# The third unit's first MLP matmul by block products, and a new step plan for three units

## The chip, the cores and the metric

The kernel runs on one core of a Trainium2 chip. The core has five engines that run at the same time and meet through semaphores: TensorE (PE, matmuls into PSUM), VectorE (DVE, elementwise), ScalarE (ACT, elementwise with activation functions), GpSimd (POOL, elementwise, slower) and SyncE (SP, whose queue here does nothing but start DMA transfers). Each engine takes its instructions in the order of its own queue. Time is device time in microseconds (us); lower is better.

## The reference

Two blocks, one after the other. The first is a gated linear recurrence over 768 steps, for 4 batches and 8 heads of 48 dimensions:

```python
f = 1.0 / (1.0 + np.exp(-f_logit))
for t in range(S):
    state = f[:, :, t, :, None] * state + np.einsum('bhd,bhe->bhde', k[:, :, t], v[:, :, t])
    y[:, :, t] = np.einsum('bhd,bhde->bhe', q[:, :, t], state)
```

Its output, laid out as x with 3072 tokens of 384 features, goes through an MLP with 2048 hidden features, all in float32:

```python
h = x @ w_in
g = h * (1.0 / (1.0 + np.exp(-1.702 * h)))
return g @ w_out
```

## The kernel before

**Units.** The 3072 tokens are cut into 12 units of 256 tokens, numbered 0 to 11 here; "the third unit" is unit 2. For each unit the kernel does the attention part and then the MLP part. The MLP of a unit runs beside the attention of the unit after it: its matmuls are the fill that keeps PE busy while DVE, ACT and POOL prepare the next step of the attention.

**Attention of a unit.** q, k and f are loaded raw, transposed (by DVE from unit 2 on, L382) into X and F, and f goes through a sigmoid (ACT L412, POOL L409). POOL multiplies neighbouring gates into `tot` (L457). Six levels of scores follow, two at a time (`levels`, L599): PE makes the scores `sc` (L466), DVE "promotes" q and k by the gates (L564), ACT copies parts aside (`Kc` L535, `Qc` L541), and DVE evacuates the scores into A (L507, L526). Then PE makes y from A and v (L584), the new states from kn and v (L695), DVE chains the states (L717 to L721), and PE adds the state's share to y (L742). ACT copies y out (L757), and DMAs on SP's queue turn it into the tile xT that the MLP reads (L815, L820).

**The MLP of units 0 and 1** is plain: h of 128 hidden features is three matmuls of 256 columns, one for each third of x (L1173, `mlp_h`), ACT applies the activation (L1177), and o is summed over blocks of four hidden tiles (L1187, added by DVE at L1243). While this goes on the weights arrive. They are loaded in 16 pairs of tiles of 64-bit floats (`fetch_weights`, L208) and turned into float32 by one ACT instruction (L252) and three DVE steps (L248, L241, L251). The loads have three buffers.

**The MLP of units 3 to 11** is by block products (`mlp_h20`, L1042). The matrix w_in is seen as 4 rows of 3 blocks, x as 3 blocks of features by 2 halves of tokens; the 24 block products are replaced by 20 products of sums of blocks, in the manner of Strassen. A product is four matmuls of 128 columns (L1079). Its left side is a sum of blocks of w_in (c1, p3, p7 and so on), made once: some stand in tiles of their own (`sums_of_w`, N_...), some overwrite a block of w_in in place (`sums_in_place`, L1002). Its right side is a sum of blocks of x, twelve sums for each unit, made by POOL (`sums_of_x`, L1037, the tiles E). The products are added up by chaining them in PSUM, by ACT copies (L1086, L1094, L1098) and by DVE adds (L1107), and activated by ACT (L1098, L1109). The products come in the order of `WHOLE` (L958): 18, 0, 7, 2, 17 and so on, of which number 18 needs the sum s7, the first that POOL makes, number 0 needs q0, the fourth, and 2 needs w, the sixth. The second matrix is done by seven products of quarters in the same manner (`mlp_o7`, L883, from unit 2 on), whose sums of w_out (T) DVE makes at L851, and whose sums of g it makes at L872 to L881.

**Unit 2 before the change** has the plain h (48 matmuls of 256 columns), run from its last block of hidden features to its first, and the o by seven products. Between its blocks stand the in-place sums (`mlp_unit`, L1224 to L1227): as soon as h has read a row of w_in for the last time, that row may be overwritten.

**Order.** PE and POOL take the instructions in the order in which the program writes them; DVE, ACT and SP too up to `fill_order.close()` (L1434), and afterwards a scheduler orders those three, except where `issue_after` puts one instruction behind another. For the attention of units 1, 2 and 3 what stands between the parts is written out by hand in `PLAN` (L1415), and inside the levels of unit 2 in `HOLES` (L276). A letter is a step: f takes the next item of the fill (for plain h the three matmuls of a tile; else one matmul of o, or one product), c is one step of a weight conversion, p begins the next conversion, w starts the next weight load on SP's queue, s takes the next of the waiting sums (`chores`), k is an idle matmul. From unit 4 on `merge` (L1304) spreads the fill by a rule.

The steps go through this function:

```python
def follow_steps(steps):
    for step in steps:
        if step == "f":
            fill.pop(0)[1]()
        elif step == "c":
            convert()
        ...
        elif step == "s":
            for job in chores[:1]:
                chores.remove(job)
                job()
```

## Time and profile before

| what | value |
|---|---|
| median of 3 runs | 575.57 us (575.4 to 575.83) |
| the profiled execution's own time | 575.35 us |
| its span | 573.6 us |
| PE busy | 563.7 us (98%) |
| DVE busy | 441.2 us (77%) |
| ACT busy | 291.7 us (51%) |
| POOL busy | 144.5 us (25%) |
| unit 2's plain h on PE (L1173) | from 142.74 to 165.39 us, with one pair of scores inside |
| unit 3's products on PE (L1079) | from 189.23 to 208.38 us, with one pair of scores inside |
| from unit to unit in the steady part | 43 us (the h of units 4 and 5 end at 251.56 and 294.56) |

A line of the order of time reads: start in us, length in us, engine, line of the kernel, instruction, output tile and input tiles, their shapes, how many instructions are merged into the line, and in brackets how long the engine had been idle before and what ended that. SPq, ACTq and PEq are the queues of those engines, where a DMA is started. Each float32 matmul shows as two PE records.

### The profile page before, as it was taken

What the parts mean: (1) busy time and instruction counts of PE and PEld (TensorE: products, weight loads), DVE (VectorE), ACT (ScalarE), POOL (GpSimd) and SP (SyncE); (2) the same over time, 40 slices, a digit from 0 to 9 for tenths busy, and PEclk for the clock granted to TensorE, in tenths of its full rate; (3) what the DMA queues carried; (4) which work ended last, traced back from release to release, by engine and by line L of the source; (5) the groups of instructions that cost most, each with busy time, mean ns of one, the idle gap of its engine ahead of it and who ended that gap; (6) DMA issues with size and microseconds to landing.
All of it is one profiled execution on the core that took longest, in us unless ns stands there. A gap on an engine that the chain in (4) does not pass through costs nothing.

```text
span 573.6 us, 18612 instructions
## 1 busy us (share of the span) xinstructions
PE 563.7 (98%) x7876; PEld 516.7 (90%) x7876; DVE 441.2 (77%) x695; ACT 291.7 (51%) x592; POOL 144.5 (25%) x227
## 2 busy tenths in 40 slices
PE   8899999999999999999999999999999999999997
PEld 7767777786899999999999999999999999999996
DVE  2899688988997786887887888886888886462294
ACT  4755553432553573564564564564564573543440
POOL 4030220419451601601601601601501601303000
PEclk9999999999999999999999999999999999999999
DMA  7869595932362452363453353453362121001000
GB/s 180 207 183 228 138 261 133 246 79 77 84 163 68 120 139 57 85 172 76 109 129 71 97 130 88 113 127 71 97 158 44 49 57 30 30 2 29 29 1 28
DMA packets 85939, 60.01 MB, mean 105 GB/s; under 512 B 33441, under 2 KB 77633, under 8 KB 85857
## 3 DMA queue, kind: packets, MB, share of 16 engines
q1 hardware_dynamic: 85328, 58.21, 40.3%
q8 instruction: 62, 1.02, 0.8%
q10 hardware_dynamic: 529, 0.62, 0.4%
q14 instruction: 20, 0.16, 0.1%
HBM read 45.16 MB, written 8.91 MB: 94 GB/s over the span
## 4 chain that ended last, share of the span: by engine, by line
PE 90%; DMA 3%; DVE 2%; ACT 2%; issue 1%; SPq 1%; ACTq 0%; DVEq 0%
PE h L1079 28%; PE o_Y L937 14%; PE o_Z L937 9%; PE h L1173 9%; PE sc L466 6%; PE o L1187 6%; PE o_X L937 5%; PE o_W L937 4%; PE y L584 2%; PE y L742 2%; PE t L394 2%; PE sc L695 2%; DMA xT<-yT 1%; DVE X L564 1%; DMA bits<-in_moe_w_in_dram 1%
## 5 line engine op out<-in xcount | busy, mean ns | idle before, releaser
L564 DVE TENSOR_TENSOR X<-X,tot 128x1024 f32<-128x1024 f32 x50 | 69.0, 1381 | 40.7 <-PE sc L466 35.1
L535 ACT COPY Kc<-X 128x512 f32<-128x512 f32 x72 | 48.3, 671 | 85.6 <-DVE X L564 71.0
L1079 PE MATMUL h<-E,w_in 128*128 128x128 f32 (+1 forms) x648 | 82.6, 276 | 0.0
L1079 PEld LDWEIGHTS h<-E,w_in 128*128 128x128 f32 x648 | 77.1, 192 | 0.5
L1107 DVE TENSOR_TENSOR g<-g,h 128x512 f32<-128x512 f32 (+1 forms) x92 | 55.4, 628 | 25.9 <-PE h L1079 18.0
L1037 POOL TENSOR_TENSOR E<-xT 128x128 f32<-128x128 f32 (+1 forms) x36 | 16.0, 454 | 231.0 <-DMA xT<-yT 231.0
L1173 PE MATMUL h<-xT,w_in 128*128 128x256 f32 x288 | 65.6, 382 | 0.2 <-DMA xT<-yT 0.2
L1173 PEld LDWEIGHTS h<-xT,w_in 128*128 128x128 f32 x288 | 53.8, 190 | 9.3 <-DMA xT<-yT 0.6
L1109 ACT ACTIVATE g<-g 128x512 f32<-128x512 f32 (+1 forms) x70 | 40.3, 588 | 34.1 <-DVE g L1107 34.1
L937 PE MATMUL o_Y<-T,S 128*128 128x192 f32 x320 | 57.6, 329 | 0.0
L937 PEld LDWEIGHTS o_Y<-T,S 128*128 128x128 f32 x320 | 52.3, 190 | 0.5
L1187 PE MATMUL o<-w_out,g 128*128 128x384 f32 x128 | 44.3, 492 | 0.0
L1098 ACT ACTIVATE g<-h 128x512 f32<-128x512 f32 (+1 forms) x70 | 37.0, 550 | 12.9 <-PE h L1079 11.0
L382 DVE STREAM_TRANSPOSE X<-raw 128x512 f32<-128x512 f32 x38 | 40.9, 1115 | 1.5 <-PE y L742 1.0
L526 DVE COPY_PREDICATED A<-masks,sc 128x256 f32<-128x256 uint32 (+1 forms) x98 | 41.9, 503 | 0.0
L757 ACT COPY yT<-y 48x256 f32<-48x256 f32 (+1 forms) x66 | 22.0, 369 | 30.0 <-PE y L742 29.5
L1079 PE MATMUL h<-E,N_c 128*128 128x128 f32 (+1 forms) x288 | 37.1, 275 | 0.0
L1187 PEld LDWEIGHTS o<-w_out,g 128*128 128x128 f32 x128 | 23.6, 190 | 14.6 <-issue 0.7
L1079 PEld LDWEIGHTS h<-E,N_c 128*128 128x128 f32 x288 | 35.1, 192 | 0.2 <-DVE osb L897 0.2
L466 PE MATMUL sc<-X,Kc 48*64 48x64 f32 x1344 | 28.3, 220 | 3.0 <-ACT Kc L535 1.2
L1177 ACT ACTIVATE g<-h 128x256 f32<-128x256 f32 x48 | 17.7, 382 | 25.5 <-PE h L1173 25.2
L466 PEld LDWEIGHTS sc<-X,Kc 48*64 48x64 f32 x1344 | 24.1, 134 | 7.3 <-ACT Kc L535 3.1
(132 smaller groups left out, 1103.4 us busy)
## 6 DMA issues: line engine op xcount, KB each, us to landing
bits<-in_moe_w_out_dram SPq DMA_DIRECT2D x8, 768.0 KB
raw<-in_f_logit_dram SPq DMA_DIRECT2D x48, 96.0 KB
raw<-in_k_dram SPq DMA_DIRECT2D x48, 96.0 KB
bits<-in_moe_w_in_dram SPq DMA_DIRECT2D x8, 576.0 KB
raw<-in_q_dram SPq DMA_DIRECT2D x44, 96.0 KB
k_tok<-z SPq DMA_DIRECT2D x64, 64.0 KB
kt<-k_tok SPq DMA_DIRECT2D x16, 256.0 KB
out_dram<-osb SPq DMA_DIRECT2D x20, 192.0 KB
```

Of the source, the lines that this page charges most:

```text
L382: copied["turned"] = nc.vector.transpose(view(out, at, [[HALF, NP], [step, R4], [R4 * step, 32]]), by_half[:, j, f].rearrange("p a (j d) - ...
L466: nc.tensor.matmul(t["sc"][h][g * HS:(g + 1) * HS, a, s, :], lhsT=t["Kc", l][rows(h), x:x + HS], rhs=rhs(h, a, g), start=True, stop=True,)
L526: moved = nc.vector.copy_predicated(out=view(A, c * HALF + at, dims), mask=mask.bitcast(U32), data=got)
L535: nc.scalar.copy(c.rearrange("p (n two m) -> p n two m", two=2, m=m), view(X, KF * SLOT, [[2 * m, SLOT // (2 * m)], [(KR - KF) * SLOT + m, ...
L564: done = nc.vector.tensor_tensor(x, x, y, ALU.mult)
L937: nc.tensor.matmul(t[name], lhsT=lhs(f), rhs=rhs(f), start=(new and i == 0), stop=(i == HF - 1), skip_group_check=True,)
L1079: nc.tensor.matmul(ph[:, t], lhsT=WA[a][:, f // 2, f % 2 * P:(f % 2 + 1) * P], rhs=E[n][b], start=(root and t == 0), stop=not goes_on, ski ...
L1098: nc.scalar.activation(to, ph, AF.Copy, scale=float(sign))
L1107: copied["sum"] = nc.vector.tensor_tensor(to, to, part, ALU.add if sign > 0 else ALU.subtract)
L1109: nc.scalar.activation(to, to, AF.Gelu_apprx_sigmoid)
L1173: nc.tensor.matmul(ph, lhsT=w_in[:, ff // 2, c, ff % 2 * P:(ff % 2 + 1) * P], rhs=xTs[n][:, c, :], start=(c == 0), stop=(c == NK - 1))
L1187: nc.tensor.matmul(t["po"], lhsT=g[ff // FG][:, ff % FG, tt * P:(tt + 1) * P], rhs=w_out[:, ff, :], start=(ff == ffs[0]), stop=(ff == ffs[ ...
```

## The change

Unit 2's h is made by twenty block products like that of the units after it. For that:

- `mlp_unit` loses its special case for unit 2; the lanes of PSUM are taken from `turns` if no unit before has set them (L1114).
- The sums of w_in must be ready before unit 2's products. The sums in their own tiles are made during unit 2's attention (steps s; `more` hands out c1, c4, p12). After it, and ahead of unit 3's first part, POOL gets the four in-place sums k, p3, p1, p14, then p15 and p16 (three instructions), and DVE gets p7, p19 and p4, behind the last state step that was written. The other three in-place sums of DVE (p9, p5, p11) are chores of unit 3's plan, behind the promotion of unit 3's level 1.
- `sums_of_x(n)` is called without its condition n > N_FILL. So POOL makes unit 2's twelve sums; unit 0 comes to the same line and makes twelve as well, which nothing reads.
- `PLAN` for the three units and `HOLES` are written anew. Around the steps that matter: unit 1's plan takes one more item of fill ahead of its last y matmuls; unit 2's first level has three conversion steps, not one, between the copies aside and the first promotion, and one, not five, ahead of the second; the load of pair 9 stands ahead of unit 2's v loads, that of pair 11 behind eight raw loads; sixteen matmuls of o of units 0 and 1 stand behind unit 2's y and not thirteen; seventeen products of unit 2 follow on one another behind unit 3's last scores.
- The third weight pair's load is written one part earlier in the opening; the sums of w_out (T) lose their tie to a transpose.

From unit 5's attention on, PE's order of work is the same in both kernels.

```diff
-    HOLES = {(N_FILL, 0): "c", (N_FILL, 1): "cccffcfcw", (N_FILL, 2): "fcp", (N_FILL, 3): "cfcf", (N_FILL, 4): "fcwwff", (N_FILL, 5): "c"}
+    HOLES = {(N_FILL, 0): "ccc", (N_FILL, 1): "c", (N_FILL, 3): "cpccfwwff", (N_FILL, 4): "ccsw", (N_FILL, 5): "f"}
...
             half(1)
             xTs[n] = xT
-            if n > N_FILL:
-                sums_of_x(n)
+            sums_of_x(n)
...
         def sub(*x):
-            with ExitStack() as order:
-                if next(made) < 2:
-                    order.enter_context(tc.issue_after(copied["turned"].ins))
-                nc.vector.tensor_tensor(*x, ALU.subtract)
+            summed.append(nc.vector.tensor_tensor(*x, ALU.subtract))
...
+        third = ("p4", "c1", "-", "a30"), ("p15", "p15", "", "p4"), ("p16", "a20", "", "a21"), ("p16", "p16", "", "a22")
...
     def sum_of_w(engine, out, x, op, y):
 
-        if op == "-":
-            with tc.issue_after(copied["promoted"].ins):
+        with ExitStack() as order:
+            if engine == nc.vector:
+                order.enter_context(tc.issue_after(copied.get("promoted", copied["state"]).ins))
+            if op == "-":
                 engine.scalar_tensor_tensor(WA[out], WA[x], -1.0, WA[y], op0=ALU.mult, op1=ALU.subtract)
+            else:
+                engine.tensor_tensor(WA[out], WA[x], WA[y], ALU.add if op else ALU.subtract)
+
+    def sums_in_place(engine):
+
+        if engine == nc.gpsimd:
+            for out, at in (("p7", "a01"), ("p19", "a12"), ("p5", "a31"), ("p9", "a11"), ("p11", "a00")):
+                WA[out] = WA[at]
+            sums = (
+                ("k", "a02", "a02", "+", "a30"), ("p3", "a02", "a11", "", "k"), ("p1", "a32", "a21", "+", "c3"),
+                ("p14", "a10", "a10", "", "c2"),
+            )
         else:
...
+            sums = (
+                ("p7", "a01", "a11", "", "c3"), ("p19", "a12", "c2", "-", "a20"), ("p9", "a11", "c4", "", "a11"),
+                ("p5", "a31", "a31", "", "c3"), ("p11", "a00", "a00", "", "c1"),
+            )
...
-            free = lanes["o"]
+            free = lanes.get("o") or [next(turns) % 4 for _ in range(4)]
...
-        if n > N_FILL:
-            return mlp_h20(n, g, before) + o
-        by_block = {}
...
-        for r in reversed(range(NGR)):
-            items += mlp_h(n, range(r * FG, (r + 1) * FG), by_block)
-            if r:
-                items.append((0, lambda r=r: sums_in_place(r), 0))
-        return items + [(0, end, 0)] + o
+        return mlp_h20(n, g, before) + o
...
     PLAN = {
         3: (
-            "ffffffsfffsfff", "fffsf", "ffffs", "fffsfsfssfffff", "s", "f", "ffsffffff", "ffffffffff", "fffffsssf",
+            "sssfcfffsssfffffsffff", "sfffffff", "", "", "fffpfsffsffsffffffffffffffff", "f", "f",
+            "ffffffffffffffffffff", "ffff",
         ),
         1: (
-            "cccwcccwkkkkk", "kkkcf", "cfccwf", "fcffcwffcffcf", "ffcc", "f", "cwc", "fcc", "ff", "cff", "", "f",
-            "wffwfffff",
+            "cccwcccwkkkkk", "kkkcf", "cfccwf", "fcffcwffcffcf", "ffcc", "f", "cwc", "fcc", "cfff", "", "pw", "fff",
+            "wffffff",
         ),
         2: (
-            "ffffff", "fcfff", "fcffffccswfwpfcsf", "cfc", "ccfcffscsffcf", "ffffsffffffff", "f", "fffcffsffff",
+            "fffff", "ffcfffpcff", "sfcfffcfcsfcpccffwwfcs", "", "fffscfff", "scffscfssfscffffcfffffffcf", "",
+            "fpfffff",
         ),
     }
...
-    while chores:
-        chores.pop(0)()
+    by_pool, by_ve, rest = [*sums_in_place(nc.gpsimd)], [*sums_in_place(nc.vector)], [*more.pop()()]
+    for x in (*by_pool, *by_ve[:2], *rest):
+        x()
...
-    of_b = [*sums_of_b()]
-    for x in sums_of_w(("c1", "c4", "p12", "p4", "p16")):
-        chores += of_b[:1] + [x]
-        del of_b[:1]
-    chores += of_b
+    chores += by_ve[2:] + [*sums_of_b()]
```

## The prediction

> **What bounds the kernel now.** I read the page first (busy shares and slices), then the waits between 57 and 210 us, then TensorE in order of time over the stage that is edited, then the queue of GpSimd (POOL) over the same stage.
>
> ```profile
> PE 563.7 (98%) x7876; PEld 516.7 (90%) x7876; DVE 441.2 (77%) x695; ACT 291.7 (51%) x592; POOL 144.5 (25%) x227
> PEclk9999999999999999999999999999999999999999
> ```
>
> TensorE (PE) is busy for 98% of the span at the full granted clock, so a time comes down only if PE gets less to do, and comes down by less wherever PE then waits. The waits from 57 to 210 us, longest first (who waited for whom: us, times, longest):
>
> ```profile
> POOL w_in L1000 <- PE h L1173: 9.8, 3, 4.8
> ...
> PE sc L466 <- DVE A L526: 0.6, 1, 0.6
> ...
> PE sc L466 <- ACT Kc L535: 0.4, 1, 0.4
> ```
>
> PE has only two of its own in 153 us; POOL's 9.8 is the old in-place sums waiting for h to be through with each row of w_in, which costs nobody. PE in order of time:
>
> ```profile
> 85.27 0.69 PE L466 MATMUL sc<-Qc,Kc 48*64 48x64 f32 x32 [0.59 <-DVE A L526]
> ...
> 142.74 4.05 PE L1173 MATMUL h<-xT,w_in 128*128 128x256 f32 x18
> 146.72 0.69 PE L466 MATMUL sc<-Qc,Kc 48*64 48x64 f32 x32
> 147.83 0.69 PE L466 MATMUL sc<-X,Kc 48*64 48x64 f32 x32 [0.42 <-ACT Kc L535]
> 148.45 17.10 PE L1173 MATMUL h<-xT,w_in 128*128 128x256 f32 x78
> 165.39 2.11 PE L937 MATMUL o_Y<-w_out,g 128*128 128x192 f32 x12
> ...
> 189.23 1.95 PE L1079 MATMUL h<-E,N_c 128*128 128x128 f32 x16
> 191.11 0.69 PE L466 MATMUL sc<-Qc,Kc 48*64 48x64 f32 x32
> ...
> 192.20 2.05 PE L1079 MATMUL h<-E,w_in 128*128 128x128 f32 x16
> ...
> 208.38 2.77 PE L937 MATMUL o_Y<-w_out,g 128*128 128x192 f32 x16
> ```
>
> The reader sees the two forms of h side by side (the records show two instructions to a matmul): unit 2's by blocks of 256 columns, 142.74 to 146.72 and 148.45 to 165.39, and unit 3's by products, 189.23 to 191.11 and 192.20 to 208.38. The two waits are 0.59 us at 85.27 and, at 146.72, scores that take 1.73 us where this pair takes 1.09 at 191.11.
>
> POOL, which must now make unit 2's sums of x:
>
> ```profile
> 127.08 1.04 POOL L457 TENSOR_TENSOR tot<-F 128x512 f32<-128x512 f32 x1 [16.62 <-DVE st L720]
> 128.20 4.16 POOL L457 TENSOR_TENSOR tot<-tot 128x256 f32<-128x256 f32 x4
> 132.43 0.22 POOL L457 TENSOR_TENSOR D<-tot 128x16 f32<-128x16 f32 x1
> 132.61 3.50 POOL L1000 TENSOR_TENSOR N_c<-w_in 128x512 f32<-128x512 f32 x2
> ...
> 144.78 1.27 POOL L1000 TENSOR_TENSOR N_p<-N_p,N_p 128x512 f32<-128x512 f32 x1
> ...
> 227.49 0.87 POOL L1037 TENSOR_TENSOR E<-xT 128x128 f32<-128x128 f32 x2 [29.67 <-DMA xT<-yT]
> 228.43 1.32 POOL L1037 TENSOR_TENSOR E<-xT,E 128x128 f32<-128x128 f32 x1
> 229.83 0.87 POOL L1037 TENSOR_TENSOR E<-E,xT 128x128 f32<-128x128 f32 x2
> ```
>
> POOL is idle 75% of the span, but not here: from 127.08 it runs without a gap to 146.05.
>
> **The change part by part.** The sum is made in this profiled execution, 575.35 us with 573.6 us of span; the median of the runs shown is 575.57, 0.22 above it.
>
> *Unit 2's h.* Off PE: 48 matmuls of 256 columns, 3.98 + 16.94 = 20.92 us. Onto PE: 80 of 128 columns, by unit 3's rows 1.88 + 16.18 = 18.06. Gain 2.86 us. With it come ten adds on VectorE (DVE) of 685 ns and ScalarE copies and activations of 10.9 instead of 6.1 us. In unit 3 the same load sits beside 18 us of products with no PE wait, and the five in-place sums that DVE made in this stretch (0.71 to 1.39 us each) are made earlier, so I price them at nothing; without that cover the bank of a product comes free late, up to one add, 0.7 us.
>
> *Old waits.* The new plan has five fewer o matmuls ahead of the scores of 85.27, but VectorE no longer waits there for a pair of w_in that landed at 76.97: its load now goes ahead of unit 2's five v loads on SP's queue (3.2 us of issue), which wait one load's issue longer and are used at 91 us. So 0.59 goes. The 0.64 at 146.72 goes into the reckoning below. Together -1.23.
>
> *Ahead of unit 2.* Since the condition on the sums of x is gone, unit 0 makes twelve too, which nothing reads, when its xT lands at 39.3 us. POOL is free until 67.0, and the twelve take 7.3 us in unit 3 (184.15 to 191.49). What they can hold up is DVE: while POOL made tot at 29.05, a conversion step took 1.32 us at 29.18 where its row is 0.55 at 36.25. Four or five steps by 0.4 to 0.6 are 1.3 to 2.7 us, against the slack of the scores at 53.25 (Kc ready at 51.86, and 0.5 us of DVE idle before): bounds 0 to 0.8, taken 0.1, since the small sums cost less (0.96 against 0.55 at 30.42). Unit 1's y comes one o matmul (0.65 us) later, its xT landed at 69.12 and PE was there at 69.57, with 0.14 of issue: +0.35. Three conversion steps instead of one stand ahead of unit 2's first promotion (71.33, freed by Qc), 0.55 + 0.96 us more, twice that if POOL is at its sums: Kc at 74.2 to 75.0 against 74.4: 0 to 0.6, taken 0.2. Levels 2 to 5: the scores are ready 0.2 to 0.5 us ahead of PE by the same rows; 0 to 1.5, taken 0.05. Sum +0.7. On SP, pair 11's load now stands behind eight raw loads of f (7.4 us of issue at 74.61): it lands near 86.5, six us after issue as pair 9's at 70.98, and is converted near 89.5; the third pair's load, written earlier, keeps its place in the queue. Nothing for both, and the 1.5 just named if pair 11 is late.
>
> *POOL's queue ahead of unit 2's products.* Now the order on POOL is tot of unit 3, four sums in place, three more of w_in, then the twelve E. tot can't start before unit 2's last state step reads the old one, as in 127.08. The sums at their own rows: 2 x 1.61 (both inputs from w_in), 2 x 1.28, 1.27, 1.67, 1.89 and 0.07 between: 11.1. tot costs 3.2 (unit 4's, 194.63 to 197.82) to 5.6 (here); 4.4, the middle, is taken, because three VectorE sums run beside it where four longer instructions did. So E begins at 127.1 + 4.4 + 11.1 = 142.6. All uncontended, 3.2 + 7 x 1.27 + 0.5, gives 139.8; the pace of 127.08 to 144.78, the same seven sums and tot beside a full DVE, 144.8. PE, 0.1 us later up to here (0.7 less 0.59), comes to the first product at 142.8: 16 o matmuls (10.6) and scores (1.09) after the scores that ended at 132.96, less the three o matmuls (1.99) that stood ahead of these and now stand behind. The first product needs the first sum only (s7); the second needs the fourth (q0), 2.75 us after E begins by the rows at 227.49: 145.35, where PE would be at 143.7. Wait 1.65; the scores behind the third product need Kc, which ScalarE now copies behind an activation of the second, +0.15: 1.8. Bounds 0 (139.8) and 3.85 (144.8); 1.8 because own rows are nearer than a stretch with other DVE work. The three sums behind the promotion (p9, p5, p11) queue on DVE ahead of the next promotion: six w_in sums at 0.71 to 1.39 bring Kc to 146.8 to 148.5, PE wanting it at 147.7 after the wait; they cost only where POOL is early.
>
> *After it.* y now follows its h by one product of o more and the next h by one less: from the end of y to the first product are 24 o matmuls (7.8) and two pairs of scores (2.18), 9.98 us, where it was 13.3. E began 8.25 us after y's end (184.15 less 175.9), q0 is needed 0.9 after the first product: no wait if E is not contended, 0.2 if so. kn's second half: its transpose waits behind one more add. +0.1 for both, 0 to 1. From unit 5's attention on PE's order is the same.
>
> Sum: -2.86 - 1.23 + 0.7 + 1.8 + 0.1 = -1.5, 573.85 in the profiled execution, 574.1 beside the median.
>
> **A rule weighed.** The row: at 151.17 two DVE sums in w_in took 2.78 us together beside POOL's, and one alone at 157.64 took 0.71. The Trainium skill (SBUF — State Buffer, Who interferes with whom) says that a DVE instruction with two SBUF inputs and a GpSimd instruction that reads SBUF exclude each other for the whole instruction. By that rule DVE's and POOL's lists add up and the time is the slow rival's, 577.7, where the rows give 574.1; the trace agrees with the rule in part, as the rival's last figures show.
>
> **Rivals.**
> *POOL in time.* E at 139.8, no wait at the products: -2.86 - 1.23 + 0.7 + 0.1 = -3.3, 572.3 beside the median, as the rest here. For it: POOL's 1.27 rows. Against: DVE is 14.5 of 16.5 us busy here.
> *POOL and DVE strictly in turn (slower).* POOL 12.6 us uncontended, and DVE's two-input work in the same stretch, 6 sums of 0.71 and two promotions of 1.23, 6.7: E at 146.4, q0 at 149.15, PE waits 5.45 from 143.7: +2.2, 577.7. Before, from 127.08 to 146.05, POOL's rows uncontended are 13.4 and DVE's two-input work 9.5, yet 19.0 elapsed, not 22.9; three fifths of DVE's work counted, which puts E at 143.7. It decides the sign from E at 144.2, and is slower by over 0.2% from 145.4.
> *The plan's head pays.* Dead sums 0.8, Kc 0.6, levels 2 to 5 at 1.0: +2.75 with 0.35 for xT, instead of 0.7: 576.1. Against: each has slack in the trace.
>
> **How the numbers follow.** About 0.2% (1.15 us) is what a measurement of this kernel tells from no change. Forecast 0.45, at 574.1, own range 573.0 to 575.4: faster by over 0.2% up to 574.4, 0.30, the rest within. POOL in time 0.2, all faster. In turn 0.25, slower in 0.22. Plan's head 0.1, slower in 0.04, within in 0.06. So faster 0.50, same 0.24, slower 0.26. The range, 572.2 to 577.3, holds the forecast's, the fast case's centre, the plan's head and the slow case up to E at 146.0; some 0.2 is left out.
>
> **What would show it.** h of unit 2 as 160 L1085 records in about 18 us; no wait at the scores near 83; the E records of unit 2 starting near 142.6 and a wait on POOL at the second product of about 1.7; twelve E records near 40 us with stretched conversions beside them. I am wrong if E begins past 145.4, if the scores before 95 wait by over 1 us, or if unit 3's products wait for E.

## The result and the profile after

The changed kernel takes 579.32 us in the median of five runs (578.0 to 580.65), the kernel before 575.57 (five runs, 575.4 to 576.06): a ratio of 1.0058, 95% interval 1.0042 to 1.0074. In a second round it was 578.99 against 574.94, ratio 1.0069 (1.0054 to 1.0083). So it is slower by 0.6 to 0.7%, where the prediction had 574.1 and no more than 577.3.

The first line of the page of the changed kernel, then what PE waited for from 30 to 215 us (who waited for whom: us in total, times, longest):

```profile
PE 561.2 (97%) x7940; PEld 515.9 (90%) x7940; DVE 450.9 (78%) x705; ACT 295.2 (51%) x594; POOL 160.7 (28%) x251
```

```profile
PE h L1085 <- POOL E L1043: 1.6, 2, 1.2
PE sc L466 <- DVE A L526: 1.5, 2, 0.8
...
PE o L1193 <- ACT g L1183: 1.1, 1, 1.1
PE h L1179 <- ACT g L1183: 0.9, 1, 0.9
PE sc L466 <- ACT Kc L535: 0.8, 2, 0.5
```

PE has 2.5 us less to do than before (561.2 against 563.7), and the span is 2.5 us longer (576.1 against 573.6): PE stands idle 5 us more than before, twice what the products took off it. Where the waits stand, in PE's order of time (start, length, instruction, in brackets the idle time ahead of it and what ended it):

```profile
48.88 2.85 PE L1193 MATMUL o<-w_out,g 128*128 128x384 f32 x8 [1.08 <-ACT g L1183]
...
75.34 0.70 PE L466 MATMUL sc<-X,Kc 48*64 48x64 f32 x32 [0.27 <-ACT Kc L535]
...
82.36 1.56 PE L1179 MATMUL h<-xT,w_in 128*128 128x256 f32 x6 [0.94 <-ACT g L1183]
...
92.48 0.69 PE L466 MATMUL sc<-Qc,Kc 48*64 48x64 f32 x32 [0.82 <-DVE A L526]
...
143.03 0.69 PE L466 MATMUL sc<-Qc,Kc 48*64 48x64 f32 x32 [0.64 <-DVE A L526]
...
146.68 1.16 PE L1085 MATMUL h<-E,N_c 128*128 128x128 f32 x8 [0.36 <-POOL E L1043]
149.03 1.16 PE L1085 MATMUL h<-E,N_c 128*128 128x128 f32 x8 [1.19 <-POOL E L1043]
...
167.39 2.77 PE L938 MATMUL o_Y<-w_out,g 128*128 128x192 f32 x16
```

Only the last three waits stand near the place where the prediction put the price of the change. The first four, 3.1 us, stand beside the attention of units 1 and 2, ahead of anything that unit 2's products need. POOL in the same execution, first beside unit 1 and then ahead of unit 2's products:

```profile
38.97 1.35 POOL L1043 TENSOR_TENSOR E<-xT 128x128 f32<-128x128 f32 x2 [5.41 <-DMA xT<-yT]
...
134.03 3.66 POOL L1003 TENSOR_TENSOR w_in<-w_in 128x512 f32<-128x512 f32 x2
...
146.16 0.88 POOL L1043 TENSOR_TENSOR E<-xT 128x128 f32<-128x128 f32 x2
```

The first line begins the twelve sums that nobody reads; the last is unit 2's E, which comes 12.1 us after the first w_in sum in place where 11.1 was predicted.

**A measure that repeats.** Executions of one kernel lie 2.6 us apart here and up to 5.2 in later rounds (before: 574.30 to 579.54), and part of that is there before the stage in question: the scores of unit 1 that wait for Kc start at 36.22 us in one trace of before and 37.19 in another, at 36.17 and 37.24 in two of the changed kernel. From these scores to the end of the span before takes 537.38 and 537.11 us, the changed kernel 539.93 and 539.96. "From the scores" below means this; it tells about 0.3 to 0.5 us from no change, where a median tells about 1. By it the change costs 2.6 to 2.9 us. The medians lie 3.7 to 4.1 apart; the rest is not in the traces behind these scores, and where it arises stays open.

### The profile page after: what moved, and what is told of

It reads as the page before. It is cut to its first block, busy times and chain, and to the rows that moved or that the text cites. A ratio compares the mean times of both kernels' runs of the same rounds, so it can differ in the third digit from the quotient of the medians.

```text
span 576.1 us, 18797 instructions
## 1 busy us (share of the span) xinstructions
PE 561.2 (97%) x7940; PEld 515.9 (90%) x7940; DVE 450.9 (78%) x705; ACT 295.2 (51%) x594; POOL 160.7 (28%) x251
## 4 chain that ended last, share of the span: by engine, by line
PE 73%; DVE 6%; POOL 3%; issue 2%; DMA 2%; ACT 1%; SPq 1%; DVEq 0%; POOLq 0%; ACTq 0%
PE h L1085 31%; PE o_Y L938 14%; PE o_Z L938 9%; PE o_X L938 5%; PE sc L466 5%; PE o_W L938 4%; PE y L584 2%; PE y L742 2%; PE sc L695 1%; DMA raw<-in_q_dram 1%; POOL w_in L1003 1%; DVE X L564 1%; DVE s L241 1%; POOL E L1043 1%; DVE T L846 1%
## 5 line engine op out<-in xcount | busy, mean ns | idle before, releaser
L1043 POOL TENSOR_TENSOR E<-xT 128x128 f32<-128x128 f32 (+1 forms) x44 | 24.0, 555 | 248.0 <-DMA xT<-yT 217.4
L1085 PE MATMUL h<-E,w_in 128*128 128x128 f32 (+1 forms) x720 | 91.8, 276 | 0.0
L1085 PEld LDWEIGHTS h<-E,w_in 128*128 128x128 f32 x720 | 85.7, 192 | 0.6
L1113 DVE TENSOR_TENSOR g<-g,h 128x512 f32<-128x512 f32 (+1 forms) x101 | 61.2, 631 | 25.1 <-PE h L1085 15.9
L1115 ACT ACTIVATE g<-g 128x512 f32<-128x512 f32 (+1 forms) x77 | 44.7, 592 | 38.6 <-DVE g L1113 38.6
L1179 PE MATMUL h<-xT,w_in 128*128 128x256 f32 x192 | 44.5, 383 | 0.9 <-ACT g L1183 0.9
L1085 PE MATMUL h<-E,N_c 128*128 128x128 f32 (+1 forms) x320 | 41.9, 276 | 1.6 <-POOL E L1043 1.6
L1179 PEld LDWEIGHTS h<-xT,w_in 128*128 128x128 f32 x192 | 35.6, 190 | 7.4 <-ACT g L1183 1.3
L1043 POOL TENSOR_TENSOR E<-E,xT 128x128 f32<-128x128 f32 (+1 forms) x55 | 32.0, 597 | 1.8
L1085 PE MATMUL h<-xT,N_p 128*128 128x128 f32 (+1 forms) x240 | 32.1, 275 | 0.0
```

Of the source, the lines that this page charges most:

```text
L1043: nc.gpsimd.tensor_tensor(e[out], e[x], e[y], ALU.add if op else ALU.subtract)
L1085: nc.tensor.matmul(ph[:, t], lhsT=WA[a][:, f // 2, f % 2 * P:(f % 2 + 1) * P], rhs=E[n][b], start=(root and t == 0), stop=not goes_on, ski ...
L1113: copied["sum"] = nc.vector.tensor_tensor(to, to, part, ALU.add if sign > 0 else ALU.subtract)
L1115: nc.scalar.activation(to, to, AF.Gelu_apprx_sigmoid)
L1179: nc.tensor.matmul(ph, lhsT=w_in[:, ff // 2, c, ff % 2 * P:(ff % 2 + 1) * P], rhs=xTs[n][:, c, :], start=(c == 0), stop=(c == NK - 1))
```

## The experiments

All eighteen, beside the medians of before on the same chip. "From the scores" compares with the changed kernel's 539.9 and before's 537.4 and 537.1. "No dead sums" is without unit 0's twelve sums of x; promotion(l) is DVE's promotion of q and k behind level l of the scores; T are the sums of w_out, "sums" p9, p5 and p11, and "head's sums" POOL's first five. The row "no dead sums, p16 late" and all below it but the last have both of these edits; from "head's sums late" on, those without the old plan have the two h back as well.

| kernel | median us | before us | ratio, 95% interval | from the scores us |
|---|---|---|---|---|
| changed kernel again | 578.99 | 574.94 | 1.0054 to 1.0083 | 539.96 |
| no dead sums | 576.95 | 574.94 | 1.0023 to 1.0046 | 538.17 |
| p16 late | 577.27 | 574.94 | 1.0024 to 1.0053 | 539.31 |
| two h back | 578.62 | 574.94 | 1.0047 to 1.0075 | 539.44 |
| before with dead sums | 577.91 | 575.76 | 1.0015 to 1.0039 | 538.76 |
| no dead sums, p16 late | 576.52 | 575.76 | 1.0005 to 1.0028 | 537.56 |
| old plan, new products | 583.77 | 575.76 | 1.0120 to 1.0154 | 544.28 |
| head's sums late | 578.24 | 575.76 | 1.0031 to 1.0060 | 539.48 |
| old plan, T late | 579.52 | 576.10 | 1.0040 to 1.0089 | 540.28 |
| T late | 580.16 | 576.10 | 1.0059 to 1.0095 | 541.44 |
| head's sums and T late | 578.90 | 576.10 | 1.0039 to 1.0077 | 538.92 |
| sums behind promotion(2) | 576.03 | 575.62 | 0.9988 to 1.0018 | 536.81 |
| head's sums, T, sums late | 577.20 | 575.62 | 1.0018 to 1.0046 | 537.97 |
| old plan, T, sums late | 577.78 | 575.62 | 1.0025 to 1.0052 | 537.83 |
| sums behind promotion(4) | 575.50 | 575.83 | 0.9985 to 1.0009 | 536.35 |
| two sums early | 574.93 | 575.83 | 0.9973 to 0.9998 | 535.77 |
| two early, three late | 575.94 | 575.83 | 0.9991 to 1.0019 | 536.49 |
| before again | 575.81 | 575.69 | 0.9989 to 1.0018 | 537.11 |

Theory A: the loss is in the plan's head, up to unit 2's last y. Rival B: it is POOL's queue ahead of unit 2's E.

**Each kernel once more, unchanged.**

> The changed kernel once more, unchanged, beside the three that follow, so that they have it on their own chip. Theory A (the loss lies in the plan's head, up to unit 2's first y) and rival B (it lies in POOL's queue ahead of unit 2's E) both expect the time of before plus 2.5 to 3.8 us, and the executions to lie further apart than before's, as they did: 2.6 us against 0.7.

> The kernel before once more, unchanged, for a second trace. In the traces of the other kernels the first scores of unit 1 that wait for Kc start between 36.1 and 37.8 us, by the opening's transfers, and from there to the end kernels that share a stage repeat to 0.1 us; the one trace of before has 36.22 and 537.38. Their medians lie 0.9 us further above before's, on average, than the part behind that point says. If the opening does it (before's is earlier), this trace has 35.5 to 36.3 us and again 537.3 to 537.5. If the one trace was not typical behind that point, it has 36.3 to 37.5 us and about 536.5.

The changed kernel's waits came again at the same places and sizes (1.08, 0.93, 0.81, 0.63, 0.35, 1.19), so they belong to the program and not to one execution. Its executions did not lie further apart than before's this time (0.6 us against 2.3), so the spread is no mark of the change. The second trace of before has its start at 37.19 us, later than the first by nearly 1 us, and 537.11 from the scores: neither of the two answers offered is the whole of it.

**The sums that nobody reads**, taken out of the changed kernel and put into the one before:

```diff
             xTs[n] = xT
-            sums_of_x(n)
+            if n >= N_FILL:
+                sums_of_x(n)
```

```diff
-            if n > N_FILL:
+            if n != N_FILL:
                 sums_of_x(n)
```

> The changed kernel without the twelve sums of unit 0 that nobody reads. Theory A: DVE's conversions beside 38.97 to 47.3 us are again as short as before the change (0.55 to 0.60 us where they took 0.78 to 0.81), Kc of that stage comes at about 46.3, the wait of 1.08 us at 48.88 before o of unit 1 is gone, and the time falls by 0.8 to 1.2 us against the changed kernel. Rival B: POOL's queue ahead of unit 2's E is the same, so it falls by no more than the 0.1 us that the prediction gave to these sums.

> The kernel before with one thing added: the twelve sums of unit 0 that nobody reads, on POOL, as the changed kernel has them. Theory A: DVE's conversions beside them grow from 0.55 to about 0.8 us, Kc and the gelu behind it come late, o of unit 1 waits about 1.1 us, and the time is 1.0 to 2.0 us above before (taking them out of the changed kernel gave 2.0). Rival B: no more than 0.1 us. If the executions spread as far as the changed kernel's, these sums also make the spread.

Without them the changed kernel is 1.8 us shorter from the scores (538.17) and 2.0 in the median; with them before is 1.4 to 1.7 longer (538.76), 0.27% in the median. The chain can be read in the lines of DVE and ACT, of the changed kernel with the sums:

```profile
41.73 1.80 DVE L560 TENSOR_TENSOR X<-X,tot 128x512 f32<-128x512 f32 x2
...
46.22 0.81 DVE L248 TENSOR_SCALAR a<-bits 128x768 int32<-128x768 uint32 x1
46.95 1.54 DVE L560 TENSOR_TENSOR X<-X,tot 128x512 f32<-128x512 f32 x2
...
47.93 0.62 ACT L535 COPY Kc<-X 128x512 f32<-128x512 f32 x1 [3.22 <-DVE X L560]
48.45 0.38 ACT L1183 ACTIVATE g<-h 128x256 f32<-128x256 f32 x1
```

and of the same kernel without them:

```profile
42.33 1.28 DVE L560 TENSOR_TENSOR X<-X,tot 128x512 f32<-128x512 f32 x2
...
46.13 0.56 DVE L248 TENSOR_SCALAR a<-bits 128x768 int32<-128x768 uint32 x1
46.60 1.29 DVE L560 TENSOR_TENSOR X<-X,tot 128x512 f32<-128x512 f32 x2
```

Beside POOL's sums a pair of promotions takes 1.54 to 1.80 us instead of 1.28. Kc behind them comes late, and the activation of h, which stands behind Kc in ACT's order, comes late with it: it begins at 48.45, though PE was done with that h at 45.86 (44.30 and 1.56 us). In the run without the sums it begins at 47.84, where the trace's first scores lie 1.06 us later, so 1.7 us earlier from them. o waits 1.08 us for that activation. (It is o of unit 0, whose MLP runs beside unit 1's attention.) Without the sums this wait is gone. In before, where they are put in, o waits 1.08 us at 49.65 in the same way. Theory A's chain is shown, and its size is above the 0.8 to 1.2 expected.

**p16's two sums behind unit 2's E**, alone and with the sums above taken out:

```diff
-    for x in (*by_pool, *by_ve[:2], *rest):
+    for x in (*by_pool, *by_ve[:2], *rest[:2]):
...
-    chores += by_ve[2:] + [*sums_of_b()]
+    chores += rest[2:] + by_ve[2:] + [*sums_of_b()]
```

(and two more steps s at the head of unit 3's plan)

> The changed kernel with the two sums of p16 behind unit 2's E on POOL instead of ahead of it; on the other engines the order stays. Rival B: E comes about 3.4 us earlier (two sums of 1.7), the waits of 0.36 and 1.19 us at the first and second product vanish, and the time falls by 1.3 to 1.7 us. Theory A: the same waits vanish, as the trace shows them, but the kernel is still 1 to 2 us slower than before, since the 2.7 us lost up to unit 2's y stay. If something else binds there (the scores, or DVE's X), the waits are replaced by a wait for it and the time falls by less than 0.7.

> The changed kernel without unit 0's twelve sums and with p16's two sums behind unit 2's E. One alone gave 2.0 us, the other 1.7. If they are two losses at two places, as theory A and rival B together have it, both gains add up: 575.2 to 575.6 us where before has 574.9, within 0.3% of it. If one of them only moves the wait that the other leaves, the time stays at 576.5 or above.

POOL's E begins at 142.99 and both waits at the products are gone, as both theories had it. But from the scores it gained only 0.6 us of the 1.5: a wait of 0.99 us took their place, the scores of 150.85 for a Kc behind promotion(4). So the third outcome, which had a limit of 0.7, is the one that came, as the trace has it; the median fell by 1.7, which is what rival B expected and more than the trace shows; of the two the trace is followed here. Together the two edits give 2.4 us from the scores, the sum of 1.8 and 0.6: two losses at two places. What is left is 0.2 to 0.5 us above before from the scores (0.8 in the median), and the products' 2.5 us are still not to be seen.

**The head of the plan: two h back between unit 2's levels**, and then POOL's first five sums moved out of them to behind unit 3's gate (POOL's part of that unit's sigmoid, L409, at 102.54 us):

```diff
-    HOLES = {(N_FILL, 0): "ccc", (N_FILL, 1): "c", (N_FILL, 3): ...
+    HOLES = {(N_FILL, 0): "ccc", (N_FILL, 1): "cf", (N_FILL, 2): "f", (N_FILL, 3): ...
```

```diff
-            "fffff", "ffcfffpcff", "sfcfffcfcsfcpccffwwfcs", "", "fffscfff", ...
+            "fff", "ffcfffpcff", "fcfffcfcfcpccffwwfc", "", "fffssssscfff", ...
```

> The changed kernel with two h of unit 1 put back between the levels of unit 2, one behind the second and one behind the third, so that the gelus of h_3 and h_4 stand ahead of the Kc and Qc that they now follow on ACT. Theory A: the wait of 0.94 us at 82.36 for the bank of h_7 goes, and the time falls by 0.5 to 0.9 us; if the next thing there (the weights' conversion ahead of sc 26) is late by as much, the wait moves to 92.48, which then grows from 0.82 to about 1.7, and the time stays. Rival B: no change.

> As the run without unit 0's sums and with p16 late, and two more edits in the head: two h of unit 1 back between unit 2's levels, and the first five sums on POOL (c3, p15, c2, p6 twice) moved from the levels of unit 2 to behind its gate, where POOL stands idle. Theory A, if POOL's sums slow DVE there: promotion(1) and promotion(3) take 1.2 instead of 2.2 us, the conversion beside them 0.6 instead of 1.6, the waits of 0.94 and 0.82 us ahead of sc 26 go, and the time is 1.0 to 1.8 us under the run that has only the first two edits. If DVE is slowed there by something else, the promotions stay at 2.2 and the time falls by 0.4 or less, as with the two h alone.

Two h back: the wait of 0.94 for a bank goes, and the one at 92.61 grows from 0.82 to 1.26; 0.5 us of gain. With the five sums late (and the two edits above) the head's waits go as theory A has it, and unit 2's y (L584) comes 1.7 us earlier from the scores, 82.47 against 84.16. Then it comes back: PE waits 1.60 us at 128.03 (h for an activation) and 1.92 at 143.37 (scores for A). And behind the second wait PE is slower for a while, with no wait: the three matmuls of o there take 3.90 us, and 2.20 in the run without the edit (142.82), while the granted clock is 0.50 from 146 to 148 us:

```profile
144.46 3.90 PE L1194 MATMUL o<-w_out,g 128*128 128x384 f32 x6
```

These 1.7 us are nearly all of the 1.9 by which the kernel is longer than without the edit. DVE in that run, a promotion of unit 2's levels first, then 104 to 121 us, where POOL now made all ten sums in one row:

```profile
83.30 1.22 DVE L564 TENSOR_TENSOR X<-X,tot 128x1024 f32<-128x1024 f32 x1
...
109.35 0.54 DVE L1236 TENSOR_TENSOR sum<-sum,o 128x384 f32<-128x384 f32 x1
...
111.30 1.62 DVE L248 TENSOR_SCALAR a<-bits 128x768 int32<-128x768 uint32 x1
...
114.39 2.02 DVE L847 TENSOR_TENSOR T<-w_out,T 128x768 f32<-128x768 f32 x1
...
124.05 0.93 DVE L847 TENSOR_TENSOR T<-w_out,T 128x768 f32<-128x768 f32 x1
```

The promotion beside which POOL no longer works takes 1.22 us; in the changed kernel its like took 2.13 (85.18). In exchange a T sum takes 2.02 where it takes 0.93 once POOL is done, and a conversion step 1.62 instead of 0.55. The price follows POOL's sums to wherever they stand beside a DVE that has no room.

**The step plan of before up to unit 2, with the new products**, and then the T sums held where they were before, in three settings:

```diff
+                        copied["turned"] = nc.vector.transpose(
...
+                if len(summed) < 2:
+                    order.enter_context(tc.issue_after(copied["turned"].ins))
```

> The changed kernel's products of unit 2 and its POOL and DVE sums behind the step plan of before up to unit 2 (steps between the levels, step plans of units 1 and 2, the load in the opening), with ten sums on POOL triggered in unit 2's plan, without unit 0's sums, and p16 late. Theory A, that the head of the new plan costs 2.7 us: it keeps the 2.86 us of the products and gives back only what remains at E and at the scores of unit 2's end, 0.5 to 1.0 us: 572.5 to 573.5 us, 0.3 to 0.4% under before. If the products themselves cost what they gain, through DVE's and ACT's work beside them, the time is that of before or above.

> The run with the step plan of before up to unit 2, with one edit: w_out's first two sums (T) are again held on DVE behind the transposes of unit 3's X, as before the change. There PE stood 5.2 us at 118.73 behind DVE, whose T sums had moved ahead of the sums of o and the X of unit 3. If those T sums are the cause, the wait goes, and the time falls from 583.8 to about 578, more if the score wait of 1.65 us at 149 goes too. If it is POOL's ten sums that slow DVE there, whatever order it keeps, 3 us or more of the wait stay.

> The changed kernel without unit 0's sums, with p16 late, the two h back between unit 2's levels, and the T sums held behind the transposes of unit 3's X. From the first scores of unit 1 (36 us) to the end the run without the last two edits took 537.6 us in its trace and before 537.4; the two h gave 0.5. If DVE's queue between 100 and 130 us is what makes the scores' A (0.64 us at 141.7) and Kc (0.99 at 149.3) late, moving 6 us of T sums out of it takes 0.5 to 1.5 us more: 535.6 to 536.6 from there, 573.5 to 574.5 us where before has 575. If the T sums only push the promotion and the w_in sums behind them later, it is 537 or more.

> The run with POOL's first five sums moved behind unit 2's gate, and the T sums held behind the transposes of unit 3's X. There the head had gained 2.1 us (the promotions 1.2 instead of 2.2) and given them back between 100 and 145, where the same sums slowed DVE's T sums to 1.6 to 2.0 us and PE waited 1.60 and 1.92. If the loss is POOL beside a DVE that has no room, wherever the two meet, taking 6 us of DVE's work out of that stretch keeps the head's gain: 535 to 536.5 us from the first scores of unit 1, 573 to 574.5 in all. If POOL's sums cost nothing there and the loss is only the order on DVE, both waits vanish and it is under 535. If the T sums are then in the way of the state's updates and the promotion, it stays at 538 or above.

The old plan keeps the head free of any wait from 37 to 118 us, and then PE stands 5.17 us, for DVE:

```profile
118.73 5.49 PE L1194 MATMUL o<-w_out,g 128*128 128x384 f32 x8 [5.17 <-DVE sum L1236]
```

There the T sums had moved ahead of the sums of o. (These four matmuls take 5.49 us, where four take 2.85 at 48.88 in the changed kernel: the granted clock is 0.50 from 118 to 124 us.) Held back, that wait is gone as expected, but the kernel still takes 579.5, since 4.24 us appear at 144.02, for the A that stands on DVE behind T, p9 and promotion(2), and 2.4 more behind it at a granted clock of 0.50 (from these scores to the products 5.55 us, and 3.14 in the run with no dead sums and p16 late). T late in the new plan is 3.9 us longer than the run without the last two edits (541.44 against 537.56): 2.1 at that A again (2.73 at 145.64, where 0.64 stood) and 1.3 in the matmuls of o behind it (3.54 us for 2.20). With the head's sums late too, T late gains 0.6 (538.92 against 539.48) where 3 or more were hoped for, and 2.75 stand at 142.48. That DVE could be eased by putting T later was wrong: in the run with no dead sums and p16 late DVE is busy for 9.8 to 10 of every 10 us from 100 to 150, but for the ten from 130 to 140 (7.4), where it stood idle 1.9 us ahead of p9. T only moved to where its lateness is PE's wait. The 0.50 is seen in six of the eighteen runs, each time with a PE wait of 1.92 to 5.17 us; it is part of their time, and no wait of theirs shows it.

**p9, p5 and p11 behind promotion(2)**, in three settings:

```diff
-                if (n, l) == (N_FILL + 1, 1):
+                if (n, l) == (N_FILL + 1, 2):
                     copied["promoted"] = done
```

(and the steps s that hand these sums out two parts later)

> The changed kernel without unit 0's sums, with p16 late and the two h back between unit 2's levels; new: the three sums that the change put behind promotion(1) of unit 3 on DVE (p9, p5, p11) stand behind promotion(2), and the T sums at the place the change gave them. Without this last edit the sum of the runs so far gives 537.1 us from the first scores of unit 1 (537.6 less 0.5 for the two h). If p9, which waits 1.9 us for POOL and holds promotion(2) and the scores' A up, makes the wait of 0.64 us at 141.7, that wait goes: 536.2 to 536.6 us from there, about 574.5 in all, 0.1% under before. If promotion(2) is late for its own reason (2.28 us beside POOL), 0.5 us or more of the wait stay and it is 537.0 or above.

> The run with POOL's first five sums behind unit 2's gate and the T sums behind unit 3's X, and now p9, p5 and p11 behind promotion(2) too. There PE stood 2.75 us at 142.48 for the A behind p9 and promotion(2). If p9's wait for POOL is the cause, 2 us or more go: 536.2 to 537 us from the first scores of unit 1, 573.8 to 575 in all. If DVE's T sums, moved to behind unit 3's X, hold promotion(1) itself, 1.5 us or more of the wait stay.

> The step plan of before up to unit 2 with the new products, the T sums late, and p9, p5 and p11 behind promotion(2). There PE stood 4.24 us at 144.02 for the same A and nowhere else behind 37 us. If p9 is the cause, 2.5 to 4 us go: 536 to 537.8 us from the first scores of unit 1, against 537.4 of before. If the cause is DVE's total work from 100 to 145 (T sums, conversions and w_in sums, all beside POOL's sums), the A is late all the same, and 2 us or more of the wait stay.

In the changed kernel DVE, ahead of the scores of 143.03, read:

```profile
137.72 1.73 DVE L1003 TENSOR_TENSOR w_in<-N_c,w_in 128x512 f32<-128x512 f32 x1 [1.90 <-POOL w_in L1003]
139.38 2.28 DVE L564 TENSOR_TENSOR X<-X,tot 128x1024 f32<-128x1024 f32 x1
```

p9 waited 1.90 us for POOL, and the promotion behind it waited with it. Moved, in the new plan the wait at the A goes altogether, 536.81 from the scores, 0.3 to 0.6 under before (the median is that of before), though 0.2 short of the least gain expected: Kc at 149.37 is then 1.17 us late. In the second setting 2.75 us go too, and 0.85 for unit 3's states and 1.85 for E appear, so that 1.0 is gained, less than expected. In the third 2.0 of 4.24 us stay, though now for the Kc ahead of the A. So p9's place was one cause. That DVE's load is the one behind it fits (DVE is busy 10.0 of 10 us from 130 to 140 and from 140 to 150 in the third), but no run took load off DVE there.

**Taking DVE's and POOL's work apart further**: p5 and p11 behind promotion(4); then POOL's c3 and p15 ahead of unit 2's gate; then c2 and p6 behind unit 3's gate as well (from the two edits, excerpts):

```diff
-                if (n, l) == (N_FILL + 1, 2):
-                    copied["promoted"] = done
+                if n == N_FILL + 1 and l in (2, 4):
+                    copied["promoted", l] = done
```

```diff
-            "cfff", "", "pw", ...
+            "cfff", "ss", "pw", ...
```

> The run with p9, p5 and p11 behind promotion(2), with one edit: p5 and p11, which the products need last (the 13th and the 20th), stand behind promotion(4) on DVE. There PE stood 1.17 us at 149.37 for a Kc behind promotion(4), and DVE had 2.6 us of these two sums ahead of it. If DVE's order makes that wait, it falls to 0.3 or less and the kernel takes 535.7 to 536.0 us from the first scores of unit 1, against 536.8 of that run and 537.4 of before: 0.2 to 0.3% under before. If the chain of scores and promotions is late without them, 0.8 us or more of the wait stay.

> As the run ahead of it, and POOL's first two sums (c3, p15), whose rows of w_in are there early, behind unit 1's states, at about 60 us, where POOL stands idle and DVE has 20% idle time, instead of behind unit 2's gate at 76.6. If POOL's sums beside DVE make the head's waits (0.68 us at 82.67, 1.07 at 91.74), promotion(1) of unit 2 takes 1.2 to 1.6 instead of 2.15 us, and 0.3 to 0.9 us of these waits go. If the two sums now slow DVE at 60 us where PE needs it (the Kc of sc 24, 0.29 us at 74.6), as much is lost there and the time stays.

> As the run ahead of it, and c2 and p6, which ran beside promotion(3) of unit 2 at 85 us, behind the gate of unit 3 at 104, as before the change. If they are what holds promotion(3) (2.3 instead of 1.2 us) and the A at 91.74, that wait goes, 0.5 to 1.0 us; what they add at 104 to 120, where POOL then runs seven or eight sums beside a full DVE, shows as a wait at unit 3's states or scores (130 to 143 us), by the run with five sums there up to 1.9 us, with two about 0.7. So 0.3 us less to 0.3 us more than the run ahead of it.

The wait of 1.17 went, and 0.69 came for a copy of ScalarE among the products (156.45): 0.5 us gained, half of what was expected. With c3 and p15 early, promotion(1) of unit 2 takes 1.23 us (76.42) where the changed kernel has 2.29, and of the head's 0.69 and 1.28 us 1.01 is left; 0.6 more. The two sums ran at 54.4 to 57.6 and not at 60: the edit ties c3 to a state step, but unit 1's states ran only from 60.75. There they stretched two promotions of unit 1 to 3.46 us together; PE waited 0.25 us for that, at 56.56. c2 and p6 later free the 1.01, and 0.68 and 1.30 appear at 127.81 and 146.84: 0.7 longer.

The middle one, two sums early, is the first version whose median interval lies under that of before: 574.93 against 575.83, ratio 0.9986 (0.9973 to 0.9998), 1.3 to 1.6 us under before from the scores. It is the best of eighteen and its interval nearly reaches 1, so the median alone would not show a gain; the trace has one. Its waits of more than 0.3 us from 30 to 215 us:

```profile
PE sc L466 <- ACT Kc L535: 1.6, 2, 1.3
PE sc L466 <- DVE A L526: 1.0, 1, 1.0
PE h L1088 <- ACT h L1095: 0.7, 1, 0.7
```

Neither POOL's E nor an activation stands there any longer; the longest is the opening's.

## Why the prediction was wrong

It had a sum of -1.5 us; the traces have +2.6. 2.7 of the 4.1 us between them lie in one step, what the new plan costs ahead of unit 2's products. By its own steps:

- **Unit 2's h, -2.86: right in mechanism, 0.4 too large.** From 146.68 to o_Y at 167.39 are 20.71 us, less the wait of 1.19 and a pair of scores (1.09): 18.4 against 18.06 predicted. "With it come ten adds on VectorE ... I price them at nothing" held in the changed kernel; only in the later versions, with other waits gone, do 0.69 us stand for a copy of ScalarE.
- **Ahead of unit 2, +0.7 and -0.59: the step that failed.** Unit 2's last y (L742) comes at 131.75; before, less the three o matmuls, at 128.99: with the start of the traces set equal, 2.8 us late and not 0.1. Of this, unit 0's dead sums, "bounds 0 to 0.8, taken 0.1", cost 1.8 by the run without them, outside their own bounds. The steps were stretched by less than was feared (0.2 to 0.5 us, where "0.4 to 0.6" stood), but they were set against the slack of the scores at 53.25. The chain that reached PE first was another: Kc late, the activation behind it in ACT's order late, o of unit 0 late. The prediction did not follow that activation.
- **In the same step, levels 2 to 5 ("0 to 1.5, taken 0.05")** have 0.94 and 0.82 us, together above the bound. The 0.94 is a PSUM bank, freed late because the plan took two h from between the levels, so that their activations stood behind three copies on ACT (two h back: this wait gone, 0.5 us gained). That the plan's new order also moves ACT's was not followed. The 0.82 is POOL beside promotion(3), 2.13 us instead of 1.23, and beside the conversion step behind it, 1.63 instead of 0.55 (with c2 and p6 moved away, the wait there is gone).
- **The old wait of 0.64 at the scores of 146.72**, counted as gone, is gone in the changed kernel (that pair, at 151.01, waits for nothing, PE having stood for E shortly before). But the pair of scores ahead of it, at 143.03, which did not wait before (140.90), now waits 0.64 us, behind p9; that the two have one size is chance. The prediction had said that p9, p5 and p11 "cost only where POOL is early". They also cost where POOL is late, for p9 waits for POOL itself and holds a promotion.
- **POOL's queue ahead of unit 2's products, +1.8: right in size, in part by luck.** The waits are 1.55 where the second product was given 1.65; tot took 4.1 us (predicted 4.4), the seven sums 12.1 (11.1). But E began at 146.16, 3.6 us later than predicted and past the 145.4 that the prediction named as a sign of being wrong, and PE came 3.5 us later too. 2.8 of both are the head's: tot waits for unit 2's last state step. For the rest the longer sums and PE's new wait of 0.64 happened to cancel. And its price was not 1.5: with E made earlier, the next Kc was late by 0.99, and 0.6 was gained.
- **After it, +0.1:** 0.5 (from 2.05 us late at unit 2's o_Y to 2.55 at the end), in pieces that no run took apart. The measured terms (-2.5, +2.8, -0.64 and +0.64, +1.55, +0.5) add up to +2.35; 0.2 of the 2.55 is in none of them.

Of the rivals the plan's head (0.1, 576.1, "each has slack in the trace") named the place, but priced it at 0.8 for the dead sums and 1.0 for levels 2 to 5, where 1.8 and 1.76 came. POOL and DVE strictly in turn (0.25, 577.7) came nearer to the reason, though the traces have DVE stretched and not strictly in turn. They were priced one by one, and they are for the most part one thing: POOL's sums slow DVE in each of the four places where the new plan put them (39 to 47, 75 to 78, 85 to 88 and 134 to 146 us). The forecast weighed this against slack at the first place and as open at the last, and passed over what it does to the promotions at the two between. The Trainium skill (SBUF — State Buffer, Who interferes with whom) says that a DVE instruction with two SBUF inputs contends with a GpSimd instruction that reads SBUF, and one with a single SBUF input outside the two-port modes does not. The traces agree in kind: in the run with the head's sums late T, with both inputs in SBUF, goes from 0.93 to 2.02 us, and the sum of o, whose second input is in PSUM, takes 0.54 beside POOL and alone. The prediction weighed the rule at POOL's last queue alone and did not ask it at the other places.

## What to carry to other kernels

- Work given to an idle engine is not free if its instructions slow a busy one: price it at every place where it will run, by the stretched rows (here 2.0 for 0.93 us), and then ask which in-order queue stands behind the stretched step. The step that was looked at had slack; the one behind it, on a third engine, had none.
- Where PE is busy 97% and a second engine is busy over 90% in the stretch, taking one PE wait away shows the next: of 1.55 us of waits for E 0.6 was kept, of 1.17 us for a Kc 0.46, of 0.96 in the head 0.58. Here, then, 0.4 to 0.6 of a wait taken away was kept; look for edits that take work off the second engine, or out of POOL's way, not for ones that change its order.
- A long wait of PE can cost more than its length: in the six runs with one of 1.92 us or more the matmuls behind it ran at half the granted clock and gave 1.3 to 2.6 us more away. Compare the durations of the matmuls behind a wait, not the waits alone.
- A condition that drops out of a diff (here n > N_FILL) can cost as much as the change was meant to bring: 1.8 us for work that nobody reads.

## What the runs showed of the hardware

- The stretch of DVE beside POOL is larger than the prediction's rows had it, and falls on the plain conversions too: the steps a and s (L248 and L241) take 0.55 us alone and up to 1.62 to 1.66 beside sums of 128x512 on POOL, more than the promotion's 1.23 to 2.29 in proportion. Sums of 128x128 (unit 0's dead ones) stretched the same steps to 0.8 only. These steps have one input; the page of the Trainium skill named above has them contend when they run in a two-port mode, and the traces don't tell the mode.
- It is not strictly in turn, by an estimate from rows. In the run with the head's sums late POOL made ten sums of 128x512 from 103.55 to 121.42, 17.9 us; alone they would take ten times 1.27 (the row at 151.37 in the run with p16 late), 12.7. DVE's steps with no input in PSUM in that time come to some 8.4 us by their rows alone (five T sums by 0.95, four conversion steps by 0.55, one and a half of L251 by 0.96). 21.1 would be strictly in turn; 5.2 of DVE's 8.4 counted, three fifths, the same share that the prediction had from before.
- The granted clock of PE falls to 0.50 with long waits. In the traces of six runs it does so from 37 us on, late in or shortly behind waits of 5.17, 4.24, 2.75, 2.73, 2.04 and 1.92 us; the three matmuls of o that follow the last five take 3.79, 3.77, 3.54, 3.89 and 3.90 us, and 2.20 where the clock stays at 1.00. It does not fall behind any wait of 1.65 us or less in the same stretch, and where two waits of 0.67 and 1.18 stand 1.2 us apart it stays at 1.00 too. No run varied the length of a wait alone, so where the limit lies, and that it is the wait itself, is not shown.
